# From the eighth pair of heads on, two units' scores back to back, and the last rows' second product one step later

## The chip, the cores and the metric

The kernel runs on one core of a Trainium2 chip. The metric is the time of one execution on the device in microseconds (us); the median of several runs counts. TensorE (PE in the tables) multiplies matrices and writes to PSUM; VectorE (DVE), ScalarE (ACT) and GpSimd (POOL) do the element-wise work; SyncE (SP) issues most DMA transfers.

## The reference

Attention with a decay bias, then two dense layers, in float32:

```python
scores = scale * np.matmul(q, k.transpose(0, 1, 3, 2))          # 4 batches, 8 heads, 576 rows, 64 columns
s_pos = np.maximum(s, 0.0)
cum = np.cumsum(s_pos, axis=-1)
bias = -(cum[:, :, :, None] - cum[:, :, None, :])
scores = np.where(causal, -1000000000.0, scores + np.minimum(bias, 0.0))
scores = scores - np.max(scores, axis=-1, keepdims=True)
attn = np.exp(scores)
attn = attn / (np.sum(attn, axis=-1, keepdims=True) + 1e-09)
x = np.matmul(attn, v)                                          # becomes 2304 tokens x 512
...
h = x @ w_in;  x = np.maximum(0.01 * h, h) @ w_out              # first layer, 512 -> 2048 -> 512
h = x @ w_in2; x = (np.maximum(h, 0.0) + np.log1p(np.exp(-np.abs(h)))) @ w_out2
```

## The kernel before

The program has two stages. In the first, some 235 us long, attention runs over 16 **pairs** of heads, numbered 0 to 15 (`p`). A pair has four **units** of score rows: unit 0 is the block of rows 384 to 511 (512 columns of scores, each head in a PSUM tile of its own), unit 1 the last 64 rows of both heads (`[]`, called `last`; 288 columns), unit 2 the block of rows 256 to 383 (384 columns), unit 3 the two blocks of rows 0 to 255 (256 and 128 columns). The second stage, the two dense layers, fills the rest of the time.

The loop over `n` takes one **step** for each unit; `i` is the step within the pair, 0 to 3. Nothing is scheduled by a planner: each engine runs its instructions in the order in which the loop writes them. In a step, before the change, the units are at these places:
- the unit of the next step: `scores()`, matmuls of K and Q and of the two decay rows BK and BQ, into PSUM tiles of which there are two for each head (`bufs=2`);
- `u0`, the unit of this step: `maxima` (VectorE: adds the mask, finds each row's maximum, writes the SBUF tile `sc`, of which there are three), then `exps` (ScalarE);
- `u1`, one step older: `divisors` (VectorE: reciprocal of the sum), then `norm` (POOL: multiplies `sc` by it);
- `u2`, two steps older: `transpose` (TensorE, into the PSUM tile `pt_t`, of which there are two), and `evacuate` (the first half of a unit's transpositions mostly by ScalarE, the second half of 384 columns by VectorE), into PA and PZ (units 0 and 1) or PB (units 2 and 3);
- `u3`, three steps older: the evacuation of its second half.

Each of these comes in two halves, one for each head (`0` and `1`). `pv` is the second product, of V with the transposed scores: for the rows of units 0 and 1 (`last` true, from PA and PZ) of the pair before it stands at the end of step 0, for units 2 and 3 (from PB) at the end of step 2. Its result, the PSUM tile `pt_v` (one buffer), is split into `xh` (ScalarE) and `xl` (VectorE).

Between the two halves of a step, `fill.step(n)` puts in half a unit of the first dense layer's work, six matmuls of 512 columns (`ps_h`, L145, or `ps_o`, L614). These **fill units** are made of two halves in successive steps, and all of them use one PSUM bank (tag `m`, one buffer): it is emptied by ScalarE (L587 into `gf`, L618 into `o`) at the end of the step of the second half. In pairs 7 to 10 a unit's halves lie in steps 0 and 1 or 2 and 3; in pairs 12 to 14 in steps 1 and 2 or 3 and 0. In pair 11 step 0 has no fill, in pair 15 step 1 has none. The weights for the fill are split into two parts on the way, by operations on all three element-wise engines that `later` puts in at fixed half steps (L108 to L133).

Of the kernel before, what the change touches and what calls it, by code (L numbers as in the profile page):

```python
# [31 lines left out]
def attn_moe_moe(ctx, tc, q, k, v, s, w1i, w1o, w2i, w2o, out):  # L32
# [10 lines left out]
    NP = B * NPAIR  # L43
# [25 lines left out]
    def later(n, fn, *args):  # L69
        todo.setdefault(clock[0] + n, []).append((fn, args))  # L70

    def tick():
        clock[0] += 1
        for fn, args in todo.pop(clock[0], ()):
            fn(*args)
# [79 lines left out]
    def attention(att, ps, fills):  # L155
# [70 lines left out]
        def parts():  # L226
            nc.vector.tensor_tensor(lo.bitcast(F32R), c1, hi, op=ALU.subtract)
            for e, x in enumerate((hi, lo)):
                nc.sync.dma_start(bb_d[:, e, :].bitcast(F32), x)
            nc.sync.dma_start(c_d, c1)  # L230
# [8 lines left out]
        def load(p, nm, queue=nc.sync, c=slice(None)):  # L239
            if p < NP:  # L240
                t, x = {"q": (Q, q), "k": (K, k), "v": (V, v)}[nm]
                queue.dma_start(t[p % 2][:, c], x[p, :, c])

        def rows(p):

            if p < NP:
                b, hs = heads(p)
                for j in range(2):
                    h, r = b * H + hs.start + j, j * D
                    move(BK[p % 2][r:r + 2], bb_d[h, :, :SB])  # L250
                    move(BQ[p % 2][r + 32:r + 34], bb_d[h, :, :SB])

        def decays(p):

            if p < NP:
                o = c_d.offset + p * 2 * S
                for j in range(2):
                    nc.sync.dma_start(M[p % 2][j * D:(j + 1) * D], bass.AP(c_d.tensor, o + j * S, [[0, D], [1, S]]))

        def columns():  # L260
            pt = ps.tile([P, 512], F32, tag="m", name="pt_c", bufs=1)
            nc.tensor.transpose(pt[:, :BH], CD[:BH], ident[:BH, :BH])
            for j in range(2):
                r = slice(j * D, (j + 1) * D)
                nc.vector.tensor_copy(CQ[r, :NP], pt[r, j:BH:2])

        def bias(p):
            if 0 < p < NP:
                m = M[p % 2]
                nc.vector.tensor_scalar(m, m, CQ[:, p:p + 1], None, op0=ALU.subtract)  # L270
                later(1, nc.gpsimd.tensor_tensor, m[:, SB:], m[:, SB:], maskl[:, SH - TL:], ALU.add)
# [116 lines left out]
        def pv(p, last):  # L388

            b, hp = divmod(p, NPAIR)  # L390
            pt = ps.tile([P, 512], F32, tag="a", name="pt_v", bufs=1)
            if last:
                q0, n = (NB - 1) * P, P + TL
                mms = [(c, PA[:, :, c, :], 0, n) for c in range(NB)] + [(NB, PZ, P, TL)]
            else:

                q0, n = 0, (NB - 1) * P
                mms = [(0, PB[:, :, 2, :P], 0, P)] + [
                    (c, PB[:, :, c, max(0, c - 1) * P:], max(c, 1) * P, (3 - max(c, 1)) * P) for c in range(NB - 1)
                ]  # L400
            for m, (c, x, o, w) in enumerate(mms):
                for j in range(2):
                    nc.tensor.matmul(  # L403
                        pt[j * D:(j + 1) * D, o:o + w], V[p % 2][:, c, j, :], x[:, j, :],
                        start=m == 0 or (not last and m == 1), stop=m == len(mms) - 1 or (not last and m == 0),
                    )
            c = slice(b * S + q0, b * S + q0 + n)

            def high():
                nc.scalar.activation(xh[:, hp, c], pt[:, :n], AF.Copy)  # L410
                later(1, low)

            def low():
                nc.vector.tensor_tensor(xl[:, hp, c], pt[:, :n], xh[:, hp, c].bitcast(F32), op=ALU.subtract)
                if not last and hp == NPAIR - 1 and b < B - 1:
                    fill.ready(b)

            later(1, high)
# [36 lines left out]
        order = [[NB - 1], [], [NB - 2], [1, 0]]  # L455
        units = [(p, ts) for p in range(NP) for ts in order]
        live = {}

        def start(n):
            if n < len(units):  # L460
                live[n] = Unit(*units[n])
                live[n].scores()

        start(0)
        for n in range(len(units) + 3):
            p, i = divmod(n, len(order))
            u0, u1, u2, u3 = (live.get(n - d) for d in range(4))
            if u3:
                u3.evacuate(1)
            start(n + 1)  # L470
            if u0:
                u0.maxima(0)
                u0.exps(0)
            if u1:
                u1.divisors()
                u1.norm(0)
            if u2:
                u2.transpose(0)
            if i == 0:
                bias(p)  # L480
                if p:
                    load(p + 1, "q")
                    load(p + 1, "k")
                    rows(p + 1)
                    decays(p + 1)
            tick()
            if n == len(units):
                fill.free = [("m", 1), ("s0", 2), ("s1", 2)]
            if n:
                fill.step(n)  # L490
            if u0:
                u0.maxima(1)
            if u2 and u0 and u0.last:
                u2.evacuate(0)
            if u0:
                u0.exps(1)
            if not n:
                parts()
                rows(1)
                decays(1)  # L500
                fill.step(n)
            if n == 1:
                columns()
            if u1:
                u1.norm(1)
            if u2:
                if not (u0 and u0.last):
                    u2.evacuate(0)
                u2.transpose(1)
            if i == 3 and p + 1 < NP:  # L510
                load(p + 1, "v")
            elif i in (0, 2) and p:
                pv(p - 1, i == 0)
            if n >= len(units):
                fill.run()
            tick()
# [118 lines left out]
    with pool("att") as att:  # L635
        attention(att, psA, make)
# [135 lines left out]
    start = {}  # L772
# [78 lines left out]
```

## Time and profile before

| what | value |
|---|---|
| runs shown | median 975.77 us (975.14 to 975.97, 3 runs) |
| profiled execution | 976.11 us, its span 974.3 us |
| TensorE busy | 967.0 us, 99% of the span |
| VectorE, ScalarE, POOL busy | 529.3, 536.1, 576.2 us |
| granted clock of TensorE | 1.00 |
| TensorE's waits between 93 and 236 us | 0.4 us on ScalarE, 0.3 us on VectorE |

Busy time is what the profile counts between an instruction's start and its modelled end; successive instructions of an engine overlap a little, so from start to start is the better measure of what one costs. A bracket at the end of a row names what the engine was idle for.

### The profile page before, as it was taken

The page shows a single profiled execution, that of the slowest core. Times are in us where ns is not written, and L with a number is a line of the kernel's source. Part 1 is how long each engine was busy: PE and PEld are TensorE (multiplying, and loading weights), DVE is VectorE, ACT ScalarE, POOL GpSimd, SP SyncE. Part 2 cuts the span into 40 slices and gives each one's busy share as a digit, 9 for nine tenths or more (in the row PEclk, how much of TensorE's full clock was granted, in tenths as well). Part 3 has the DMA queues.
Part 4 walks back from the last instruction along what each step waited for, and adds up shares of the span by engine and source line. Part 5 has one row for each costly group of instructions (what it writes and reads, how often), then busy time and mean ns, then how long its engine had stood idle before and what let it go on. Part 6 is the DMA issues. An engine that isn't in the chain of part 4 may idle for free.

```text
span 974.3 us, 14738 instructions
## 1 busy us (share of the span) xinstructions
PE 967.0 (99%) x5268; PEld 785.0 (81%) x5268; DVE 529.3 (54%) x1140; ACT 536.1 (55%) x1119; POOL 576.2 (59%) x568
## 2 busy tenths in 40 slices
PE   9999999999999999999999999999999999999998
PEld 6666777777998888888888888888888888888886
DVE  7888566554122222222325358666688868764434
ACT  6888677565453333333344456766656655654452
POOL 7788556443454444344535556777677767774554
PEclk9999999999999999999999999999999999999999
DMA  6444452420621111111102110211011101100202
GB/s 230 156 160 140 134 170 77 143 73 23 218 85 43 44 44 43 35 52 44 44 23 65 44 44 22 65 39 48 22 44 45 64 23 44 44 0 1 87 22 87
DMA packets 37774, 68.06 MB, mean 70 GB/s; under 512 B 3018, under 2 KB 20298, under 8 KB 37700
## 3 DMA queue, kind: packets, MB, share of 16 engines
q1 hardware_dynamic: 37268, 66.36, 21.2%
q8 instruction: 42, 0.69, 0.3%
q10 hardware_dynamic: 432, 0.75, 0.2%
q14 instruction: 32, 0.26, 0.1%
HBM read 59.01 MB, written 8.09 MB: 69 GB/s over the span
## 4 chain that ended last, share of the span: by engine, by line
PE 97%; DVE 1%; POOL 1%; ACT 0%; issue 0%; DMA 0%; DVEq 0%; POOLq 0%
PE ps_h L145 41%; PE ps_out L752 37%; PE pt_s L311 5%; PE pt_v L403 4%; PE pt_t L372 4%; PE ps_o L614 3%; PE pt_t L367 1%; PE pt_s L297 1%; PE pt_w L191 0%; POOL sc L355 0%; DVE sc L332 0%; POOL wil L133 0%; DVE acc L764 0%; DVE PA L386 0%; ACT sc L344 0%
## 5 line engine op out<-in xcount | busy, mean ns | idle before, releaser
L151 POOL TENSOR_TENSOR gl<-gf,gh 128x512 fp32r<-128x512 f32 (+2 forms) x148 | 182.6, 1234 | 150.5 <-ACT gh L150 140.8
L145 PE MATMUL ps_h<-xh,wih 128*128 128x512 f32 (+2 forms) x640 | 237.5, 371 | 0.0
L145 PE MATMUL ps_h<-xh,wil 128*128 128x512 f32 (+2 forms) x640 | 235.8, 368 | 0.0
L145 PE MATMUL ps_h<-xl,wih 128*128 128x512 f32 (+2 forms) x640 | 235.6, 368 | 0.0
L764 DVE TENSOR_TENSOR acc<-ps_out,acc 128x512 f32<-128x512 f32 (+1 forms) x115 | 73.8, 657 | 164.2 <-PE ps_out L752 164.2
L711 POOL TENSOR_TENSOR t<-e,t 128x512 f32<-128x512 f32 (+1 forms) x80 | 112.2, 1403 | 72.2 <-DVE t L710 71.4
L355 POOL TENSOR_SCALAR sc<-sc,st 128x512 f32<-128x512 f32 (+4 forms) x160 | 89.0, 567 | 82.7 <-DVE st L351 76.2
L145 PEld LDWEIGHTS ps_h<-xh,wil 128*128 128x128 f32 x640 | 120.5, 188 | 19.7
L145 PEld LDWEIGHTS ps_h<-xh,wih 128*128 128x128 f32 x640 | 120.6, 188 | 19.3
L145 PEld LDWEIGHTS ps_h<-xl,wih 128*128 128x128 f32 x640 | 120.6, 189 | 19.1
L695 ACT ACTIVATE gf<-ps_h 128x512 f32<-128x512 f32 (+2 forms) x68 | 37.3, 548 | 177.4 <-PE ps_h L145 174.6
L150 ACT ACTIVATE gh<-gf 128x512 fp32r<-128x512 f32 (+2 forms) x148 | 86.1, 582 | 49.1 <-DVE gf L721 48.5
L752 PE MATMUL ps_out<-woh,gl 128*128 128x512 f32 x289 | 112.5, 389 | 0.0
L752 PE MATMUL ps_out<-wol,gh 128*128 128x512 f32 x289 | 112.4, 389 | 0.0
L752 PE MATMUL ps_out<-woh,gh 128*128 128x512 f32 x289 | 112.4, 389 | 0.0
L123 POOL TENSOR_TENSOR wm<-wm,wt 128x512 int32<-128x512 int32 x64 | 85.2, 1332 | 30.7 <-DVE wm L120 30.7
L344 ACT ACTIVATE sc<-sc,st 128x512 f32<-128x512 f32 (+2 forms) x144 | 83.4, 583 | 31.4 <-DVE st L350 20.1
L752 PE MATMUL ps_out<-gh,wol 128*128 128x512 f32 (+2 forms) x272 | 99.1, 364 | 0.0
L752 PE MATMUL ps_out<-gh,woh 128*128 128x512 f32 (+2 forms) x272 | 99.1, 364 | 0.0
L752 PE MATMUL ps_out<-gl,woh 128*128 128x512 f32 (+2 forms) x272 | 99.0, 364 | 0.0
L710 DVE TENSOR_SCALAR t<-e 128x512 f32<-128x512 f32 (+1 forms) x80 | 44.2, 552 | 98.2 <-ACT e L701 98.2
L114 DVE TENSOR_SCALAR wm<-wm 128x512 f32<-128x512 f32 x64 | 38.1, 596 | 92.7 <-ACT wm L108 92.6
(112 smaller groups left out, 1677.1 us busy)
## 6 DMA issues: line engine op xcount, KB each, us to landing
rawi<-in_moe_w_in SPq DMA_DIRECT2D x32, 512.0 KB
rawo<-in_moe_w_out SPq DMA_DIRECT2D x32, 512.0 KB
K<-in_k SPq DMA_DIRECT2D x15, 432.0 KB
V<-in_v SPq DMA_DIRECT2D x16, 320.0 KB
Q<-in_q SPq DMA_DIRECT2D x15, 320.0 KB
out<-acc SPq DMA_DIRECT2D x17, 256.0 KB
M<-c_d SPq DMA_DIRECT2D x30, 144.0 KB
part<-o SPq DMA_DIRECT2D x12, 256.0 KB
```

The costliest lines, as they stand in the source:

```text
L123: nc.gpsimd.tensor_tensor(m, m, t, op=ALU.add)
L145: nc.tensor.matmul(ps, a, b, start=kk == 0 and n == 0, stop=kk == KD - 1 and n == 2)
L150: nc.scalar.activation(gh, gf, AF.Copy)
L151: nc.gpsimd.tensor_tensor(gl, gf, gh.bitcast(F32), op=ALU.subtract)
L311: nc.tensor.matmul(self.ps[j][:, c], x[r, t * P:(t + 1) * P], y[r, :(t + 1) * P], start=x is Q[i], stop=x is bq,)
L344: nc.scalar.activation(x, x, AF.Exp, scale=-1.0, bias=self.stat(0, e + self.last), accum_out=self.stat(1, e))
L355: nc.gpsimd.tensor_scalar(x, x, self.stat(2, e), 1.0, op0=ALU.mult, op1=ALU.mult)
L372: nc.tensor.transpose(pt[:, c * P:(c + 1) * P], sc[:, j, c * P:(c + 1) * P], ident)
L710: nc.vector.tensor_scalar(t, e, 1.0, -1.0, op0=ALU.add, op1=ALU.add)
L711: nc.gpsimd.tensor_tensor(t, e, t, op=ALU.subtract)
L752: nc.tensor.matmul(u, a, v, start=f == 0 and m == 0, stop=f == G - 1 and m == 2 and j == k - 1)
L764: nc.vector.tensor_tensor(d[..., x], o[..., x], d[..., x], op=ALU.add)
```

## The change

It touches only the loop over `n`, and only from `p` = 7 on (`wide`), nine pairs. In step 1 no scores are started; in step 2 the scores of unit 2 and of unit 3 are started one behind the other, and unit 2 is `u0` of that same step. The second product of the last rows (`last` true) goes from the end of step 0 to the end of step 1. In step 2 the divisors and the first `norm` of unit 1 go ahead of the maximum of unit 2; in step 0 the first evacuation of `u2` goes ahead of the second `exps` of `u0`, as it did already where `u0` is the last rows' unit. The rest of the order follows from these.

```diff
         order = [[NB - 1], [], [NB - 2], [1, 0]]
         units = [(p, ts) for p in range(NP) for ts in order]
         live = {}
+        wide = 7
 
         def start(n):
-            if n < len(units):
+            if n < len(units) and n not in live:
                 live[n] = Unit(*units[n])
                 live[n].scores()
...
             if u3:
                 u3.evacuate(1)
-            start(n + 1)
+            late = wide <= p < NP
+            if late and i == 2:
+                start(n)
+                u0 = live[n]
+            if not late or i != 1:
+                start(n + 1)
+            if u1 and late and i == 2:
+                u1.divisors()
+                u1.norm(0)
             if u0:
                 u0.maxima(0)
                 u0.exps(0)
-            if u1:
+            if u1 and not (late and i == 2):
                 u1.divisors()
                 u1.norm(0)
...
             if u0:
                 u0.maxima(1)
-            if u2 and u0 and u0.last:
+            soon = u2 and u0 and (u0.last or late and i == 0)
+            if soon:
                 u2.evacuate(0)
             if u0:
                 u0.exps(1)
...
             if u2:
-                if not (u0 and u0.last):
+                if not soon:
                     u2.evacuate(0)
                 u2.transpose(1)
             if i == 3 and p + 1 < NP:
                 load(p + 1, "v")
-            elif i in (0, 2) and p:
-                pv(p - 1, i == 0)
+            elif i in (late, 2) and p:
+                pv(p - 1, i != 2)
```

TensorE's order in pair 12, from the last matmul of the fill in step 0 on. `pt_t` are transpositions, `pt_v` the second product, `pt_s` scores, `ps_o` a fill unit; the numbers tell the buffers' uses apart, and L614 has become L624. Before:

```order
L614 MATMUL ps_o_2317<-gh_2179,wol_1401 128x512
L372 MATMUL pt_t_2375<-ident_84,sc_2249 128x128 x3
L403 MATMUL pt_v_2379<-PA_99,V1_98 64x192 x8
L403 MATMUL pt_v_2379<-PZ_100,V1_98 64x64 x2
L311 MATMUL pt_s_2397<-K0_87,Q0_85 128x384
L311 MATMUL pt_s_2398<-K0_87,Q0_85 128x384
L311 MATMUL pt_s_2397<-BK0_91,BQ0_89 128x384
L311 MATMUL pt_s_2398<-BK0_91,BQ0_89 128x384
L372 MATMUL pt_t_2409<-ident_84,sc_2301 128x128 x3
L614 MATMUL ps_o_2416<-gh_1875,woh_1063 128x512
```

And with the change:

```order
L624 MATMUL ps_o_2317<-gh_2179,wol_1401 128x512
L372 MATMUL pt_t_2375<-ident_84,sc_2251 128x128 x3
L372 MATMUL pt_t_2391<-ident_84,sc_2301 128x128 x3
L624 MATMUL ps_o_2397<-gh_1874,woh_1063 128x512
...
L372 MATMUL pt_t_2408<-ident_84,sc_2301 128x128 x3
L403 MATMUL pt_v_2412<-PA_99,V1_98 64x192 x8
L403 MATMUL pt_v_2412<-PZ_100,V1_98 64x64 x2
L311 MATMUL pt_s_2425<-K0_87,Q0_85 128x384
L311 MATMUL pt_s_2426<-K0_87,Q0_85 128x384
L311 MATMUL pt_s_2425<-BK0_91,BQ0_89 128x384
L311 MATMUL pt_s_2426<-BK0_91,BQ0_89 128x384
L311 MATMUL pt_s_2431<-K0_87,Q0_85 128x256
```

The second product and the scores of unit 2 have gone from between the transpositions of step 0 and those of step 1 to behind step 1's; the scores of units 2 and 3 now follow each other.

ScalarE's order in step 0 of pair 12, from the exponentials of unit 0 (`sc_2341`) to the maker of `xh`. L384 evacuates transpositions, L127 copies a weight, L618 (now L628) empties the fill's bank. Before:

```order
L344 ACTIVATE sc_2341,st_2342<-sc_2341,st_2342 128x512 x2
L384 ACTIVATE PB_101<-pt_t_2349 128x3x128
L127 ACTIVATE woh_2390<-wm_2261 128x512
L618 ACTIVATE o_2392<-ps_o_2317 128x512
L410 ACTIVATE xh_67<-pt_v_2379 128x192
```

And with the change:

```order
L344 ACTIVATE sc_2341,st_2342<-sc_2341,st_2342 128x512
L384 ACTIVATE PB_101<-pt_t_2349 128x3x128
L344 ACTIVATE sc_2341,st_2342<-sc_2341,st_2342 128x512
L127 ACTIVATE woh_2379<-wm_2261 128x512
L628 ACTIVATE o_2381<-ps_o_2317 128x512
```

The evacuation has gone ahead of the second exponential, and the maker of `xh` has gone to the next step; the weight copy and the store keep their places behind the exponentials. On POOL and on the DMA queue nothing moves.

## Rows read from the trace of the kernel before

**Rows 1.** The page: the chain that ended last, share of the span.

```profile
PE 97%; DVE 1%; POOL 1%; ACT 0%; issue 0%; DMA 0%; DVEq 0%; POOLq 0%
```

**Rows 2.** Windows of pairs 9, 12, 15: length, busy us (count), clock, DMA.

```profile
core 0: us, PE busy (x) PEld busy (x) DVE busy (x) ACT busy (x) POOL busy (x), PEclk, DMA share, GB/s
125.50:141.40 15.90, 15.90 (x119) 11.38 (x119) 10.65 (x38) 11.37 (x31) 9.45 (x14) 1.00 0.53 163
171.79:187.69 15.90, 15.90 (x119) 11.37 (x118) 8.56 (x35) 9.76 (x27) 7.98 (x13) 1.00 0.41 136
219.48:235.00 15.52, 14.82 (x113) 10.95 (x113) 9.01 (x38) 10.04 (x28) 7.82 (x15) 1.00 0.01 5
```

**Rows 3.** TensorE's order of time in pair 12: start, busy us, instruction, count.

```profile
174.22 0.49 PE L372 MATMUL pt_t<-ident,sc 128*128 128x128 f32 x3
...
176.20 0.92 PE L311 MATMUL pt_s<-K,Q 64*128 64x384 f32 x4
...
177.22 0.55 PE L372 MATMUL pt_t<-ident,sc 128*128 128x128 f32 x3
177.53 0.47 PE L614 MATMUL ps_o<-gh,woh 128*128 128x512 f32 x1
...
179.00 0.49 PE L372 MATMUL pt_t<-ident,sc 128*128 128x128 f32 x3
179.42 0.70 PE L311 MATMUL pt_s<-K,Q 64*128 64x256 f32 x4
...
180.45 0.66 PE L372 MATMUL pt_t<-ident,sc 128*128 128x128 f32 x4
180.86 0.47 PE L614 MATMUL ps_o<-gh,woh 128*128 128x512 f32 x1
...
184.31 1.13 PE L311 MATMUL pt_s<-K,Q 64*128 64x512 f32 x4
...
185.60 0.66 PE L367 MATMUL pt_t<-ident,sc 128*128 128x128 f32 x4
```

**Rows 4.** TensorE at the tail of attention, no scores left.

```profile
234.01 0.50 PE L614 MATMUL ps_o<-gh,woh 128*128 128x512 f32 x1 [0.36 <-ACT o L618]
...
239.01 0.49 PE L372 MATMUL pt_t<-ident,sc 128*128 128x128 f32 x3
239.25 0.48 PE L614 MATMUL ps_o<-gh,woh 128*128 128x512 f32 x1
```

**Rows 5.** ScalarE's order of time in pair 12 and at the tail.

```profile
174.87 0.47 ACT L384 ACTIVATE PB<-pt_t 128x384 f32<-128x384 f32 x1
175.47 0.63 ACT L127 ACTIVATE woh<-wm 128x512 fp32r<-128x512 f32 x1
176.01 0.58 ACT L618 ACTIVATE o<-ps_o 128x512 f32<-128x512 f32 x1
...
233.38 0.58 ACT L618 ACTIVATE o<-ps_o 128x512 f32<-128x512 f32 x1
```

**Rows 6.** ScalarE in step 0 of pairs 9, 11 and 13.

```profile
128.44 0.72 ACT L344 ACTIVATE sc<-sc,st 128x512 f32<-128x512 f32 x1
...
159.65 0.72 ACT L344 ACTIVATE sc<-sc,st 128x512 f32<-128x512 f32 x1
...
190.77 0.47 ACT L384 ACTIVATE PB<-pt_t 128x384 f32<-128x384 f32 x1
```

**Rows 7.** TensorE's transpositions in step 0 of pairs 7 and 11.

```profile
95.93 0.49 PE L372 MATMUL pt_t<-ident,sc 128*128 128x128 f32 x3
...
157.94 0.87 PE L372 MATMUL pt_t<-ident,sc 128*128 128x128 f32 x6
```

**Rows 8.** VectorE's evacuation in step 0 of pair 15.

```profile
222.44 0.56 DVE L386 COPY PB<-pt_t 128x384 f32<-128x384 f32 x1 [0.64 <-PE pt_t L372]
```

**Rows 9.** POOL in step 0 of pairs 7 and 12.

```profile
96.04 0.92 POOL L355 TENSOR_SCALAR sc<-sc,st 128x256 f32<-128x256 f32 x2 [0.43 <-DVE st L351]
...
98.46 0.82 POOL L355 TENSOR_SCALAR sc<-sc,st 128x256 f32<-128x256 f32 x2
...
174.17 1.27 POOL L123 TENSOR_TENSOR wm<-wm,wt 128x512 int32<-128x512 int32 x1
```

## The prediction

> **What bounds the kernel now.** I read the chain that ended last first: TensorE holds 97% of it [rows 1], so only what lengthens or shortens TensorE's own row counts. The second view is the windows of the attention stage, one window for each pair of heads, cut where the scores of a pair's second unit begin. A pair takes 15.9 us, TensorE is busy for all of it, and its granted clock is 1.00, the upper level of 2.4 GHz [rows 2]. The other engines are busy for 8 to 12 us of the 15.9, but their work is tied to TensorE's step by step, and the reader is to look for how late each result comes before TensorE asks for it. So the third view is TensorE's order of time in pair 12, and the next ones are the three other engines at the places where the change draws TensorE's requests together.
>
> **What the change gives back.** Three things go away in each of the nine pairs 7 to 15, all read in pair 12 [rows 3]. In the tables S is a block of scores by its columns, T a group of transpositions, V a second product, F a half fill unit of six matmuls.
> First, the joint between S384 and S256. A lone S512 takes 184.31 to 185.60, 1.29; a lone S384 takes 176.20 to 177.22, 1.02; so 128 columns cost 0.27, and lone blocks of 256 and 128 would take 0.75 and 0.48, together 1.23. Side by side they take 179.42 to 180.45, 1.03. A joint between two score blocks is thus worth 0.20, and the change makes one more.
> Second, the transpositions that now follow S384: three take 177.22 to 177.53, 0.31, to the next fill. Behind a fill three take 0.24 [rows 4]. They will stand behind other transpositions, so 0.07 goes.
> Third, the way from transpositions into S256: 179.00 to 179.42, 0.42. One transposition follows another after 0.11 (four instead of three move the fill from 0.31 to 0.41), so three should take 0.33; 0.09 goes.
> The sum is 0.36 a pair and 3.2 us for nine. The ends: 0.20 a pair (1.8 us) if the joint alone counts, and 0.47 (4.2 us) if the last transposition before scores also hides wholly (0.20 in place of 0.09). I take 0.36, since each of its three parts is read between neighbours of the same kinds.
>
> **What it takes.** The second product of the last rows (V) and S384 now stand no longer between the transpositions of step 0 and those of step 1. On TensorE F, T3, V, S384, T3, F becomes F, T3, T3, F. In pair 12 the first F ends at 174.22, 2.43 behind the pair's start [rows 2, 3]; step 1's first transposition came at 177.22 and its fill at 177.53. Now the transposition is due at 2.43 + 3 x 0.11 = 2.76 and the fill at 2.43 + 0.24 + 0.33 = 3.00, some 2.7 us sooner. What they wait for doesn't come sooner: step 0's work on the other engines starts with the mask-and-maximum of the pair's first unit, which needs a score buffer that the last transposition of the step before frees, so it hangs on TensorE's own place in step 3, which stays. I price the waits one by one, with 0.05 us from the end of an instruction to TensorE's start: at the tail of attention, where no scores are left between, a store that ends at 233.38 + 0.58 = 233.96 lets its fill start at 234.01, and the trace books 0.36 of TensorE waiting there [rows 4, 5]. That row is the change's new situation in small.
> - **The fill's bank.** Fill units share one PSUM bank. In pairs 12, 13 and 14 step 0 ends one unit and step 1 begins the next, so the fill must wait for ScalarE to empty the bank. In pair 12 the store stands behind a weight copy (L127) that waits for POOL's addition, which runs from 174.17 to 175.44; the store ends at 176.01 + 0.58 = 176.59 [rows 5, 9]. The fill starts at 176.64 instead of 171.79 + 3.00 = 174.79: 1.85. In pair 13 nothing but the exponentials are ahead; the evacuation now goes before the second one, and the store takes the place at 190.77, so the fill starts at 190.77 + 0.58 + 0.05 = 191.40 instead of 187.69 + 3.00 = 190.69: 0.71 [rows 2, 6]. Pair 14 repeats it: 0.71.
> - **The transposition buffer.** There are two of them, and step 1's first transposition needs step 0's first one evacuated by ScalarE. The change puts that evacuation (0.47 [rows 5]) before the second exponential. In pairs 12 to 15 it is done in time. In pair 9 two operations of a weight split stand ahead, and the place is 128.44: ready at 128.44 + 0.47 + 0.05 = 128.96, due at 125.50 + 2.76 = 128.26: 0.70. In pair 11, step 0 has no fill: transpositions begin at 157.94, and six of them and 0.07 later step 1's is due, 158.67; the evacuation behind the copy L592 takes the place at 159.65 and is ready at 160.17: 1.50 [rows 2, 6, 7]. Pair 10 has pair 11's copy but a fill to cover it: 0.11 by the same sum. In pair 15, where step 1 has no fill, its second three are due at 219.48 + 2.43 + 0.66 = 222.57, while VectorE's evacuation of step 0's second three ends at 222.44 + 0.56 = 223.00: 0.48 [rows 2, 8].
> - **The normalised scores.** In pair 7 POOL is late by a fill's subtraction: the first two normalisations end at 96.04 + 0.92 = 96.96, while the third transposition is due at 95.93 + 0.33 + 0.22 = 96.48: 0.53. Then a fill of 1.47, and the other two end at 98.46 + 0.82 = 99.28, due at 97.01 + 0.03 + 1.47 + 0.22 = 98.73: 0.60 [rows 3, 7, 9].
> - Pair 8 has its inputs in time by the same sums.
> Together 1.85 + 0.71 + 0.71 + 0.70 + 1.50 + 0.11 + 0.48 + 1.13 = 7.2 us.
> The ends: 3.3 us if only the three bank waits are real, and 9.2 if each of the ten waits costs 0.2 more (restart, an evacuation pushed on). The sums go by rows at the very instructions, so I take 7.2.
> **Moves at no cost.** The third unit's scores are now made in the step that uses them, so VectorE's maximum of that unit waits for TensorE. Behind it stand the xl subtraction, which frees the bank of the next second product, and the unit's other maximum, which frees the buffer for S512. S384 ends 1.02 into the step, and three VectorE operations, none longer than the 0.56 of an evacuation of the same 384 columns, end by 2.7 [rows 3, 8]; S512 comes 4.89 behind S256, which itself now stands 0.82 into the step, so at 5.7 [rows 3]. POOL's order and the DMA queue's do not change. Divisors taken ahead in step 2 belong to a unit that is done.
> **Sum.** 7.2 - 3.2 = +4.0 us. The profiled execution took 976.11 (its span 974.3 and 1.8 around it), so 980.1; the median of the runs shown is 0.34 lower, so **979.7 us**.
>
> **The rivals.**
> *The waits are covered, and only the gain is left (faster).* The place is ScalarE in step 0: had it emptied bank and buffer within 2.8 to 3.0 us of the pair's start, 975.8 - 3.2 = 972.5. For it speaks that ScalarE idles in half of the rows. Against it: the ends above are fixed by the exponential that waits for VectorE and by POOL's addition, and none of those instructions leaves its place. It decides if the nine pairs together wait less than 1.3 us.
> *Only the bank waits (no change).* 3.3 - 3.2 = +0.1, so 975.9. This needs the transpositions' inputs in pairs 7, 9, 11 and 15 to be earlier than in the trace, by 0.5 to 1.5 us.
> *The just-in-time scores hurt too (slower still).* If VectorE or ScalarE lose the 3.0 us of room in step 2, each pair loses more; 0.5 in each is 4.5 more, 984. Pairs with weight-split work there are the likeliest.
> *The clock falls.* A TensorE that stands idle for longer could be granted 1.2 GHz; one whole pair at half clock costs at most 15.9, 995.6. The window at the end of attention holds 0.70 us of waiting (15.52 against 14.82 busy) at 1.00 [rows 2], so I give it 1 in 100. The Trainium skill (TensorE: Matmul & The Clock Gate, HAM oscillation) speaks for this rival: it says that waits between bursts of matmuls can drop TensorE to half its clock; the trace so far agrees only in that no drop follows short waits.
>
> **How the numbers follow.** The forecast has 0.80, covered waits 0.07, bank waits alone 0.08, just-in-time harm 0.04, the clock 0.01. A measurement of this kernel can tell about 0.2%, 1.95 us, from no change. So faster 0.07, within 0.2% 0.08, slower 0.85. The likeliest case's own range, from the ends of its terms without both extremes at once, is 977.6 to 982.0; to leave out no more than 2 in 10 I take 977.0 to 982.3.
>
> **What would show it.** In the profile after: S384 runs straight into S256 and the block S384, S256, S128 lasts about 1.85 us, against 2.05 apart. TensorE's waits, 0.7 us over these pairs before, come to about 7 to 8 us: on ScalarE's L628 and L597 (bank) near 3.3, on ScalarE's L384 near 2.3, on POOL's L355 near 1.1, on VectorE's L386 near 0.8 with the old one. Pair 8 is shorter than before by 0.36, pair 12 longer by 1.5. The forecast is wrong if the bank of the next unit proves free when step 1's fill arrives, or if the waits are there but one swallows the next.

## The result and the profile after

| | median | range, runs | ratio to before, 95% interval |
|---|---|---|---|
| before | 975.75 us | 975.14 to 976.07, 6 | |
| with the change | 980.3 us | 980.1 to 982.57, 6 | 1.0052 (1.0039 to 1.0064) |

The change makes the kernel 4.55 us slower; 979.7 was forecast, +4.0. The profiled execution has a span of 978.3 us against 974.3. In it pair 7 starts 0.78 us sooner (at 92.56 instead of 93.34), and that difference arises in the first two pairs, which the change doesn't touch; the profiles of experiments 1 to 6, which leave those pairs alone too, have pair 7 begin 0.1 to 0.9 us sooner. So over pairs 7 to 15 and the tail behind them the change loses 4.8.

The windows of pairs 7, 8, 12 and 13 after, cut as in [rows 2]:

```profile
core 0: us, PE busy (x) PEld busy (x) DVE busy (x) ACT busy (x) POOL busy (x), PEclk, DMA share, GB/s
92.56:109.52 16.96, 16.33 (x119) 11.37 (x118) 10.65 (x37) 11.00 (x31) 9.00 (x15) 1.00 0.43 138
109.52:125.28 15.76, 15.76 (x119) 11.51 (x118) 9.59 (x37) 10.33 (x31) 8.71 (x13) 1.00 0.51 158
173.24:190.68 17.44, 15.82 (x118) 11.50 (x117) 8.56 (x35) 9.80 (x27) 7.97 (x13) 1.00 0.35 116
190.68:207.00 16.32, 15.84 (x119) 11.48 (x118) 8.56 (x35) 9.81 (x27) 6.31 (x12) 1.00 0.33 104
```

Pair 8, which was to have no wait, takes 15.76, and the clock stays at 1.00. Pair 12 takes 17.44 against 15.90 [rows 2], and its TensorE is no longer busy for all of it. From pair start to pair start the nine pairs change by +0.90, -0.34, +0.50, -0.09, +1.26, +1.54, +0.43, +0.39 and +0.22 us (pair 15 with the tail), together +4.8.

TensorE's order of time in pair 12, to be held against [rows 3]:

```profile
175.65 0.81 PE L372 MATMUL pt_t<-ident,sc 128*128 128x128 f32 x6
178.09 0.50 PE L624 MATMUL ps_o<-gh,woh 128*128 128x512 f32 x1 [1.62 <-ACT o L628]
...
181.58 0.92 PE L311 MATMUL pt_s<-K,Q 64*128 64x384 f32 x4
...
182.50 0.60 PE L311 MATMUL pt_s<-K,Q 64*128 64x256 f32 x4
...
183.43 0.66 PE L372 MATMUL pt_t<-ident,sc 128*128 128x128 f32 x4
```

And ScalarE's at the same place, against [rows 5]:

```profile
175.06 0.47 ACT L384 ACTIVATE PB<-pt_t 128x384 f32<-128x384 f32 x1
175.60 0.72 ACT L344 ACTIVATE sc<-sc,st 128x512 f32<-128x512 f32 x1
176.23 0.19 ACT L344 ACTIVATION_READ_ACCUMULATOR sc<-sc,st 128x1 f32 x1
176.93 0.63 ACT L127 ACTIVATE woh<-wm 128x512 fp32r<-128x512 f32 x1 [0.51 <-POOL wm L123]
177.46 0.58 ACT L628 ACTIVATE o<-ps_o 128x512 f32<-128x512 f32 x1
```

The six transpositions begin at 175.65, and the fill that would follow 0.57 later, as it does in pair 8 (112.14 to 112.71), starts at 178.09, 0.05 behind the store's end (177.46 + 0.58 = 178.04): 1.87 lost. The store stands behind a weight copy that waits for POOL, as before the change. The gain is in the same rows: S384 to the transpositions behind S128 takes 181.58 to 183.43, 1.85.

The waits of TensorE from 85 to 240 us, before and after:

```profile
PE ps_o L614 <- ACT o L618: 0.4, 1, 0.4
PE pt_t L372 <- DVE PA L386: 0.3, 1, 0.3
```

```profile
PE pt_t L372 <- ACT PB L384: 2.1, 2, 1.4
PE ps_o L624 <- ACT o L628: 2.0, 2, 1.6
PE pt_t L372 <- POOL sc L355: 0.5, 2, 0.3
PE ps_h L145 <- ACT gf L597: 0.5, 1, 0.5
PE ps_h L145 <- ACT o L628: 0.5, 1, 0.5
PE pt_t L372 <- DVE PB L386: 0.4, 1, 0.4
PE pt_t L372 <- DVE PA L386: 0.3, 1, 0.3
```

Three kinds are new: the bank of the fill (L628, L597), the buffer of the transpositions (L384 and L386 of PB), POOL's normalisation (L355). This view counts from the modelled end of the matmul before, so it shows 1.6 where starts show 1.87.

### The profile page after: what moved, and what is told of

Same layout as the page of the kernel before. It is cut to its first block, busy times and chain, and to the rows that moved or that the text cites. A ratio compares the mean times of both kernels' runs of the same rounds, so it can differ in the third digit from the quotient of the medians.

```text
span 978.3 us, 14748 instructions
## 1 busy us (share of the span) xinstructions
PE 965.2 (99%) x5268; PEld 785.2 (80%) x5268; DVE 530.1 (54%) x1140; ACT 536.1 (55%) x1119; POOL 575.9 (59%) x568
## 4 chain that ended last, share of the span: by engine, by line
PE 94%; DVE 2%; POOL 2%; ACT 1%; issue 1%; DMA 0%; DVEq 0%; POOLq 0%
PE ps_h L145 40%; PE ps_out L762 37%; PE pt_s L311 5%; PE pt_v L403 4%; PE pt_t L372 3%; PE ps_o L624 3%; PE pt_t L367 1%; DVE sc L332 1%; POOL sc L355 0%; PE pt_s L297 0%; ACT sc L344 0%; DVE PA L386 0%; DMA M<-c_d 0%; POOL wil L133 0%; DVE acc L774 0%
## 5 line engine op out<-in xcount | busy, mean ns | idle before, releaser
L355 POOL TENSOR_SCALAR sc<-sc,st 128x512 f32<-128x512 f32 (+4 forms) x160 | 88.7, 565 | 83.7 <-DVE st L351 76.2
```

Source lines behind the costliest of these rows:

```text
L355: nc.gpsimd.tensor_scalar(x, x, self.stat(2, e), 1.0, op0=ALU.mult, op1=ALU.mult)
```

## The experiments

The ratio is to the kernel before on the same chip, whose median there was 975.46 us (first four) or 975.70 (last three), with its 95% interval. The 980.3 of the whole change was measured apart from these, so differences to it are good to about 1 us; differences of pairs are read from the traces.

**1. Only the scores moved.** The second product of the last rows is back at the end of step 0.

```diff
-            elif i in (late, 2) and p:
+            elif i in (0, 2) and p:
```

> The second product of the last rows is put back to the end of step 0; the third unit's scores stay in front of the fourth's. Theory (waits of step 1's inputs, because second product and scores left the place between the transpositions): 1.57 us of second product stand between them again, so the waits of the changed kernel, 7.8 us over pairs 7 to 15 by its trace, fall to about 0.2 (pair 12's bank alone), and one joint of 0.20 us a pair is left as gain, 1.8 us: about 974.1. Rival A (the scores made in the step that uses them cost the time): the loss stays, about 979 to 980. Rival B (the gain is the number of changes between kinds of matmul, which is here that of the kernel before): 975.8, no change.

Measured: 974.15 us, ratio 0.9986 (0.9977 to 0.9995). Its waits of TensorE from 85 to 240 us are those of the kernel before, the first of them the tail's (at 232.00):

```profile
PE ps_o L624 <- ACT o L628: 0.4, 1, 0.4
PE pt_t L372 <- DVE PA L386: 0.3, 1, 0.3
```

So scores made in the step that uses them cost nothing, and rival A falls. Rival B is not tested by this run, because its premise was wrong: counted in the orders, TensorE changes its kind of matmul 18 times a pair before, 17 times here, 16 times with the whole change and 18 times in experiment 2, so an equal price for every change would forecast this gain too. Against an equal price speaks the kernel before itself: pair 11 lacks one half fill unit between two groups of transpositions, and with it two changes, and takes 14.50 us against pair 12's 15.90. These 1.40 are just six fill matmuls at 0.233 from start to start (173.05 to 173.98 for four), so those two changes cost nothing. So only changes to or from the scores or the second product can cost, and the joint saves one of these.

Pair 8 takes 15.88, against 16.10 before and 15.76 with the whole change: 0.22 for the joint, 0.12 for the rest. Pair 12 gains only 0.02. Its fill starts at 175.28, 0.05 behind the store's end, 0.47 behind its transpositions instead of 0.30: the 0.2 of bank wait that was expected there, which the view doesn't list.

**2. Only the second product moved.** The scores of unit 2 are started in step 1 again, and the divisors keep their old place.

```diff
-            if late and i == 2:
-                start(n)
-                u0 = live[n]
-            if not late or i != 1:
-                start(n + 1)
-            if u1 and late and i == 2:
-                u1.divisors()
-                u1.norm(0)
+            start(n + 1)
...
-            if u1 and not (late and i == 2):
+            if u1:
```

> The third unit's scores go back to step 1, at its beginning; the second product of the last rows stays at the end of step 1. Theory of waits: 1.02 us of scores stand between the transpositions of step 0 and 1, so of the waits about 0.7 (pair 12's bank) and 0.4 (pair 11's buffer) are left, and no joint between scores is gained: about 976.8. Rival A (scores just in time): these are as early as before, so no loss at all, 975.8. Rival C (the later second product itself harms, by the bank of its result or by the later xh and xl): as much as the whole change, 979 to 980.

Measured: 977.72 us, ratio 1.0023 (1.0014 to 1.0032). Slower, as the theory of waits has it, but by 0.9 us more than its sum; neither rival's time came. Pairs 8, 9, 10, 13 and 14 are within 0.02 us of the kernel before, so the later second product costs nothing by itself. TensorE's order of time in pair 11, VectorE's, and a row of the waits of TensorE's weight loads (PEld, 90 to 165 us):

```profile
157.80 0.87 PE L372 MATMUL pt_t<-ident,sc 128*128 128x128 f32 x6
158.61 1.51 PE L311 MATMUL pt_s<-K,Q 64*128 64x384 f32 x3
159.54 0.44 PE L311 MATMUL pt_s<-BK,BQ 64*128 64x384 f32 x1
159.96 0.48 PE L311 MATMUL pt_s<-K,Q 64*128 64x384 f32 x1
...
160.55 0.55 PE L372 MATMUL pt_t<-ident,sc 128*128 128x128 f32 x3
```

```profile
158.79 0.68 DVE L332 CUSTOM_DVE_ANT_0 sc<-pt_s,mask 128x512 f32<-128x512 f32 x1
159.40 0.08 DVE L332 DVE_READ_ACCUMULATOR2_ANT st<- 128x1 f32 x1
```

```profile
PEld pt_s L311 <- DVE st L332: 0.9, 2, 0.6
```

S384 takes 158.61 to 160.55, 1.94 instead of 1.02: the second head's score tile, which unit 0 used last, is free only when VectorE has read its maximum at 159.47. In pair 7 it takes 1.60. These 1.5 us I had left out; with them and 0.70 in pair 12, which was expected, the waits are 2.2. The wait view of TensorE's matmuls doesn't show them, since the row at 158.61 counts as busy through the wait (1.51 for three matmuls); from start to start they show, and in the weight loads' view in part. With the whole change S384 stands late enough, so moving the scores is what keeps this wait away.

**3. The fill's halves moved.** The whole change, with the fill of step 2 of pair 11 run a step later.

```diff
-            self.run()
+            if n != 46:
+                self.run()
```

> The whole change, but the fill of one step (step 2 of pair 11) is left out there and so runs one step later, which moves the halves of the fill units of pairs 12 to 14 from steps 1-2 and 3-0 to steps 0-1 and 2-3; nothing is computed less. Theory: the bank waits of pairs 12, 13 and 14 (1.9, 0.8, 0.7 us in the changed kernel's trace) go, and pair 15's 0.6 too, since its step 1 gets a fill: 980.3 - 4.0 = 976.3. Rival (the waits are for the transpositions' own inputs and only booked on the bank): they stay, 980.

Measured: 976.53 us, ratio 1.0011 (1.0002 to 1.0019). 3.8 us come back, as expected, and no wait for the fill's bank is left in the view:

```profile
PE pt_t L372 <- ACT PB L384: 2.1, 2, 1.4
PE pt_t L372 <- POOL sc L355: 0.8, 3, 0.3
PE pt_t L372 <- DVE PA L386: 0.3, 1, 0.3
```

The sum came out, its terms only in part. Against the whole change pair 12 gives back 1.73 and pair 13 0.78, but pair 14 only 0.22, because there POOL's normalisation is the next to be late (the third wait for it, at 206.67), and pair 15 0.37. The tail, which I hadn't counted, gives 0.59: its fill no longer waits for the store of [rows 4]. So the rival falls in pairs 12 and 13, and that 3.8 met 4.0 was in part luck.

**4. The evacuation earlier still.** The whole change, with step 0's first evacuation right behind the transpositions' call.

```diff
                 u2.transpose(0)
+                if late and i == 0:
+                    u2.evacuate(0)
...
-            if soon:
+            if soon and u0.last:
                 u2.evacuate(0)
```

> The whole change, but in step 0 the evacuation of the first transpositions goes right behind the first exponential, ahead of what the half step puts on ScalarE (a weight split's two operations in pair 9, a fill's copy in pairs 10 and 11). Theory: pair 9's 0.86 and pair 10's 0.24 go; pair 11's 1.5 stays nearly whole, since POOL's normalisations are the next to be late there (0.96 at the first, 0.51 at the second half): 980.3 - 1.1 = 979.2. Rival (the evacuation is not what these pairs wait for): 980.3.

Measured: 978.96 us, ratio 1.0037 (1.0025 to 1.005), 1.3 us less than the change. Pairs 9 and 10 take 0.37 and 0.35 less than before, so their waits are gone whole. The transposition buffer has gone from TensorE's waits, and in pair 11 POOL has come in its place:

```profile
158.64 0.52 PE L372 MATMUL pt_t<-ident,sc 128*128 128x128 f32 x3 [0.90 <-POOL sc L355]
```

**5. The evacuation back.** The whole change without its third part.

```diff
-            soon = u2 and u0 and (u0.last or late and i == 0)
+            soon = u2 and u0 and u0.last
```

> The whole change, but step 0's first evacuation goes back behind the second exponential, as in the kernel before. Theory: step 1's first transposition then waits for it in every pair: by the rows of the kernel before it ends 3.55 us into pairs 10 to 15 (4.13 in pair 9, 3.88 in pair 8, 4.76 in pair 7) where it is due at 2.76. Pairs 13 and 14, which wait 0.72 for the bank anyway, lose only 0.1 more, pair 12 nothing; pairs 8 to 11 lose 0.6 to 0.9 more each, pair 15 0.2, pair 7 some 1: 980.3 + 4.5 = 984.8, at least 983. Rival (the evacuation's place doesn't matter, the pairs wait for bank and POOL): 980.3.

Measured: 983.7 us, ratio 1.0081 (1.0067 to 1.0094). A loss of 3.4 over the change; I had summed 4.5. The part of the change that moves the evacuation is worth that much, and without it the other two would cost 8. TensorE's waits, and the rows of VectorE, ScalarE and TensorE in pair 11:

```profile
PE pt_t L372 <- DVE PB L386: 4.0, 4, 1.4
PE pt_t L372 <- ACT PB L384: 3.2, 4, 0.8
PE pt_t L372 <- POOL wm L123: 0.8, 1, 0.8
PE ps_o L624 <- ACT o L628: 0.6, 1, 0.6
```

```profile
162.20 0.55 DVE L386 COPY PB<-pt_t 128x384 f32<-128x384 f32 x1
...
163.04 0.90 ACT L384 ACTIVATE PB<-pt_t 128x384 f32<-128x384 f32 x2
...
162.90 0.52 PE L372 MATMUL pt_t<-ident,sc 128*128 128x128 f32 x3 [1.42 <-DVE PB L386]
```

By pairs the expectation failed in 7, 9 and 11, which lose less than 0.1 over the change where 0.6 to 1 was summed. I had step 1's first transposition wait for ScalarE's evacuation in every pair. In these three it starts before that evacuation begins (162.90 against 163.04) and 0.15 behind the end of VectorE's (162.75), so it goes into the buffer that VectorE empties, as the view's four DVE rows say; pair 8 is the fourth.

**6. Each part where it is covered.** Scores side by side in all nine pairs, the second product in step 1 in all but 7 and 11, with the edit of 3 and, in the same seven pairs, that of 4; in 7 and 11 the evacuation stands where it did in the kernel before.

```diff
             late = wide <= p < NP
+            far = late and p not in (7, 11)
...
-            elif i in (late, 2) and p:
+            elif i in (far, 2) and p:
```

> Scores side by side in pairs 7 to 15 as in the change, but the last rows' second product goes to step 1 only in the pairs where the waits can be taken away (8, 9, 10, 12 to 15); in 7 and 11 it stays in step 0. With the moved halves of the fill units and the evacuation right behind the first exponential. Theory: seven pairs gain 0.35, two gain 0.20, and 0.2 of waiting is left (pair 12): 975.5 - 2.65 = 972.8, faster than the kernel before by 0.27% and than the one with only the scores moved by 1.3 us. Rival (some further wait turns up, as the next late input): 974 or more.

Measured: 972.12 us, ratio 0.9964 (0.9952 to 0.9977): faster than both kernels. Its windows of pairs 10, 12 and 13:

```profile
139.78:155.32 15.54, 15.54 (x119) 11.47 (x118) 11.00 (x38) 11.65 (x32) 9.68 (x14) 1.00 0.41 128
168.24:183.99 15.75, 15.75 (x118) 11.40 (x118) 8.60 (x35) 9.85 (x27) 7.99 (x13) 1.00 0.37 124
183.99:199.52 15.53, 15.53 (x118) 11.47 (x117) 8.64 (x35) 9.40 (x26) 5.53 (x11) 1.00 0.46 148
```

15.53 against 15.89 to 15.90 in the kernel before, the 0.36 of the forecast. Pair 12 keeps 0.2: its three transpositions from 172.71 on take 0.61 to the second product instead of 0.42, while POOL's normalisations run (172.18 to 173.67). The 0.7 below the expected time are mostly the wait for the fill's bank at the tail [rows 4], which has gone with the halves' move. From the transpositions to the fill the tail took 0.88 before (to 234.01) and takes 0.27 here:

```profile
233.13 0.52 PE L372 MATMUL pt_t<-ident,sc 128*128 128x128 f32 x3 [0.34 <-DVE PA L386]
```

```profile
228.31 0.52 PE L372 MATMUL pt_t<-ident,sc 128*128 128x128 f32 x3 [0.34 <-DVE PA L386]
228.58 0.48 PE L628 MATMUL ps_o<-gh,woh 128*128 128x512 f32 x1
```

**7. The scores side by side from pair 1 on.** As 6, with `wide = 1` and the second product moved where it was in 6.

> As the kernel before this one in the list, with the scores side by side from pair 1 on instead of 7. Theory: pairs 5 and 6, which have fills, gain 0.20 each; pairs 1 to 4 have none, so only second product and six transpositions stand between a step's scores and the next, and what the joints give there (0.8) may go to waits for POOL and for DMA, of which these pairs already have 1.1 us: between 972.0 and 973.5. Rival (joints count alike everywhere): 971.6.

Measured: 974.61 us, ratio 0.999 (0.9981 to 0.9999), 2.5 us slower than 6 and outside what I expected. Against 6, pairs 1 to 4 lose 0.12, 0.32, 0.92 and 0.80, pair 5 gains 0.18, and pair 6 loses 0.51. Pairs 1 to 4 have no fill in these steps, and with S384 gone only the second product stands between step 0's transpositions and step 1's; pair 4 from 51.07 on, and pair 6:

```profile
54.49 0.52 PE L372 MATMUL pt_t<-ident,sc 128*128 128x128 f32 x3 [0.18 <-DVE PB L386]
55.99 0.68 PE L372 MATMUL pt_t<-ident,sc 128*128 128x128 f32 x3 [0.98 <-POOL sc L355]
...
84.88 0.52 PE L372 MATMUL pt_t<-ident,sc 128*128 128x128 f32 x3 [0.40 <-DVE PB L386]
```

The joint is there too (S384 takes 0.93 to S256 in pair 4, 56.60 to 57.53), but the scores were cover, and the cover was worth more. Pair 6 has fills and loses all the same, so a fill alone doesn't tell whether a pair is covered; there the transposition waits for VectorE's evacuation.

## Why the prediction was right

*What bounds it.* Right: what TensorE's row gained and lost is the whole difference; the chain that ended last is still 94% TensorE.

*The gain.* 0.36 a pair was forecast; pair 8, without waits in either kernel beyond the one for a store in both, gained 0.34, and in experiment 6 pairs 8, 9, 10, 13 and 14 gained 0.35 to 0.37. The joint, forecast at 0.20, measured 0.19 to 0.22 alone in experiment 1, but for pair 12 and its bank wait. The other two parts, forecast at 0.16, show in pair 8's rows: six transpositions take 0.57 to the fill, where two groups of three took 0.42 and 0.31. 3.1 us in nine pairs for the 3.2.

*The waits.* With 0.35 of gain in each, the differences of the pairs give 1.25, 0, 0.85, 0.26, 1.61, 1.89, 0.78, 0.74 and 0.57 us for pairs 7 to 15, together 8.0; forecast were 1.13, 0, 0.70, 0.11, 1.50, 1.85, 0.71, 0.71 and 0.48, together 7.2. Each term is short by 0.03 to 0.15. The sums took 0.05 from any instruction's end to TensorE's start, read at a fill that waits for a store. That fits the fills (0.05 and 0.06 in pairs 12 to 14), but a transposition starts 0.14 to 0.15 behind the evacuation that frees its buffer: in pair 11 the evacuation ends at 159.81 + 0.47 = 160.28 and the transposition starts at 160.42. Behind a wait the first fill matmul also takes 0.34 to the next instead of 0.31. The shortfall is the difference between 4.0 and 4.8 in the traces. That the two profiled spans differ by just the forecast 4.0 is luck: the first two pairs, which the change doesn't touch, were 0.78 shorter in the second. Experiment 3 gives back the bank waits of pairs 12 and 13, experiment 4 those for the buffer in pairs 9 and 10. A slip in the range: the list has nine waits, not ten, so 0.2 more for each makes 9.0.

*No cost.* That the scores made just in time hurt nothing was shown by experiment 1. The later second product costs nothing by itself, by five pairs of experiment 2. That nothing else of the moves costs anything fits the sum; it wasn't tried apart.

*The rivals.* Covered waits, bank waits alone and just-in-time harm each fell; the bank waits are 3.4 of 8.0. The granted clock stayed at 1.00, the upper level, in the windows with the longest waits, and at 0.999 over the execution, so the clock rival fell. The drop that the Trainium skill warns of (TensorE: Matmul & The Clock Gate, HAM oscillation) no run here shows, with waits of up to 1.9 us.

*What was to show it.* The block of scores took the forecast 1.85, pair 12 grew by 1.54 for 1.5, pair 8 shrank by 0.34 for 0.36. The waits in the wait view came to 6.3 where I had said 7 to 8: the view begins at a matmul's modelled end and loses some 0.25 at each. I compared two measures there; the sums went by starts.

## What to carry to other kernels

Work that stands between a producer and its consumer on the bound engine is cover, and moving it takes the cover along: before work is drawn together for a cheaper joint, write down when each input of what moves up is ready, and on which engine and behind what it hangs. Here 0.35 us a pair was to be had for 0 to 1.9 us of waiting; the same move pays once it is made only where inputs are early, or after the late ones (a bank shared by successive units, an evacuation behind unrelated copies) are brought forward. A wait can hide in a row that counts as busy and be missing from the wait view; starts against starts show it. And which of two buffers an instruction gets decides what it waits for: read it from the trace of each pair (experiment 5).

## What the runs showed of the hardware

Two blocks of 64-row score matmuls side by side cost 0.19 to 0.22 us less than the same blocks with other matmuls between them, in eight of nine pairs (experiment 1; the ninth has a wait); I had it from slopes alone. A half fill unit between transpositions costs nothing beyond its six matmuls (1.40 us, pairs 11 and 12 before).

VectorE's short divisor operation (L350) can be held until a POOL operation ends. In experiment 7, VectorE and then POOL:

```profile
52.48 0.16 DVE L350 TENSOR_SCALAR st<-st 128x4 f32<-128x4 f32 x1
...
54.76 0.47 DVE L350 TENSOR_SCALAR st<-st 128x2 f32<-128x2 f32 x1
```

```profile
53.93 1.27 POOL L133 TENSOR_TENSOR wil<-wm,wih 128x512 fp32r<-128x512 f32 x1
```

The second, on fewer elements, ends at 55.23, POOL's subtraction at 55.20. Over the first 250 us of all nine traces 103 of 576 rows of L350 are longer than 0.3 us, and each of them ends 0.01 to 0.04 us behind a POOL operation. On a single column (128x1) the same line takes 0.14 to 0.16 in the middle of a POOL subtraction, so it isn't held there. The Trainium skill (SBUF — State Buffer, SBUF: two separate sides) says that VectorE and POOL share a pair of ports that one of them holds for a whole instruction; these rows agree for two and four columns, but no run here took POOL's operation away to show it.
